# Attention and a two-layer MLP on one core: Silu table behind batch 1's Exp, eight banks for the first two tiles, a third q and k buffer

## The chip, the cores and the metric

One core of a Trainium2 chip runs the whole computation. The metric is the device time of one execution in microseconds (us), the median of several runs. The engines work side by side, each through its own list of instructions in order: TensorE (PE in the profile: matmuls; PEld: its weight loads), VectorE (DVE), ScalarE (ACT: activations and copies), GpSimd (POOL: here it issues nearly all loads) and SyncE (SP: here it issues the stores). Matmuls write into PSUM, which has 8 banks of 128 x 512 fp32 values.

## The reference

Sliding-window causal attention over 8 batches of 8 heads, 576 positions and 64 dimensions a head, then an MLP with Silu over the 4608 resulting tokens:

```python
batch, n_heads, seq, head_dim = (8, 8, 576, 64)
scores = scale * np.matmul(q, k.transpose(0, 1, 3, 2))
rel = pos[:, None] - pos[None, :]
mask = (rel >= 0) & (rel < 64)
scores = np.where(mask, scores, -1000000000.0)
attn = np.exp(scores - max);  attn = attn / sum
attn_out = np.matmul(attn, v)                 # -> x: 4608 tokens of 512
h = x @ w_in                                  # 512 -> 2048
out = (h * (1.0 / (1.0 + np.exp(-h)))) @ w_out   # 2048 -> 512
```

## The kernel before

**Tiles.** A batch has 9 blocks of 64 positions (`NB`), so there are 72 blocks, and the MLP takes them in 9 tiles of 512 tokens (`TT`, `NTT`), eight blocks each. Matmuls are in bf16 with fp32 sums.

**Attention.** For a block of 64 queries the keys are the block itself and the one before. q and k are loaded with the cast to bf16 by POOL and turned so that the head dimension lies on partitions. Batch 0 does this with TensorE: rows land in `natbs`, are transposed into PSUM (`turn_first`, L284) and copied to `qt[0]`, `kt[0]` (`lift`, L291). All later batches load into `nats` (`load_rows`, L241, four loads for each of four parts) and are turned by VectorE (`turn_blocks`, L248) into `qt[b % NK]`, `kt[b % NK]`. `NK = 2` is the number of q and k buffers; a batch's turning waits until the last scores of batch `b - NK` are done. v goes to `vv[b % NV]`, three buffers (`load_v`, L255), with two copies that shift half of it to the other partitions (`shift_v`, L299 and L301).

After batch 0, blocks are taken in *visits* of three (48 scores and 48 values matmuls), later four (64 and 64): scores into four banks (`scores`, L334), four Exp on ScalarE (`expo`, L344), four mask products on VectorE (`masking`, L349), values (`values`, L368) into two or three banks, then reciprocal (L375), product (L378) and a transpose into `bridge` (L382, L387), which holds x for the MLP. Batch 0 is done in six smaller units (L313, L321, L341, L355).

**MLP.** The first layer of a tile (`first_layer`, L393) makes 16 parts of 128 hidden features, four matmuls each, into one bank; ScalarE's Silu (L399) takes the bank to a `g` buffer in SBUF. Tile 0 also covers the ninth block of batch 0, in pieces of 192, 384, 256 and 320 columns; tile 1 goes in pieces of 192, 256 and 448 columns, and small copies (L402) bring over what tile 0 made for it. The second layer (`second_layer`, L405) is 4 x 16 matmuls of 512 columns into four banks; for tile 0 the hidden part is the outer loop, so all four banks fill together, and every eight matmuls need another block of w_out. An output copy (L411, on ScalarE or VectorE) and a store on SP (L415) follow.

**Order of the work.** The instructions are not issued as the code runs. `Plan` collects operations with a class (its rank in `rank`, `rank0` or `ahead`), an estimated duration on each engine that may do them, dependencies, a latency, a `gate` and a pool of PSUM banks; `Plan.run` plays them through in time and writes each engine's list in the order that comes out. An engine on the chip then follows its list strictly, waiting at each instruction for what it needs. Estimates therefore set the order, not the time. Pools: `at` banks 0 to 3, `pv` 4 and 5, `mp` and `pv3` 4 to 7, `all` all eight. The scores of a visit use `at`; values of batch 1 use `at` while few have been made and `pv` later; the first layer and the second use `mp`, until all values are made, and then all eight.

**Around the change.** ScalarE needs a table for Exp and another for Silu; a load of one replaces the other. A `prime` operation, a Silu over four values, draws the Silu table in behind batch 0's last Exp (L688). Later loads stand in front of the first Exp or Silu that needs another table. `add_first_batch` loads batch 0, `add_batch_qk` and `add_four` the others, `add_unit` makes batch 0's units, `add_visit` the visits, `add_tile` a tile's MLP. Instructions on PE in the order of the program before, from tile 0's second layer on, with the number of matmuls:

```
L405 x23, L334 x48, L405 x13, L334 x48, L405 x9, L334 x48, L405 x5, L368 x48, L405 x14,
L393 (192) x8, L368 x48, L393 (192) x16, L368 x48, L393 (192) x32, (256) x56, (448) x8,
L334 x48, L405 x21, L368 x48, L334 x48, L405 x27, L368 x48, L405 x2, L334 x64, L405 x14, L393 (512) x64
```

Of the kernel before, what the change touches and what calls it, by code (L numbers as in the profile page):

```python
# [122 lines left out]
def kernel(ctx, tc, q, k, v, w_in, w_out, out):  # L123
# [35 lines left out]
    nats = [keep.tile([128, 2 * S], BF16, name=f"nat{i}") for i in range(NN)]  # L159
    natbs = [keep.tile([128, S], BF16, name=f"natb{i}") for i in range(NNB)]  # L160
    qt = [keep.tile([128, NP * S], BF16, name=f"qt{i}") for i in range(NK)]
    kt = [keep.tile([128, 64 + NP * S], BF16, name=f"kt{i}") for i in range(NK)]
    vv = [keep.tile([128, H * NB + 1, D + 2], BF16, name=f"vv{i}") for i in range(NV)]
# [13 lines left out]
        rank=dict(prime=-8, early=-10, one=-9, edge=-8.5, first=-9, dma=-1, ld0=-1, dma0=-8.7, st=-2, silu=-3, out=-2, pv=0, s=1, moe=99, warm=200, turn=2,  # L177
                  norm=0, inverse=0, bridge=0, exp=1, mask=1, lift=2, block=2, shift=2, cast=4, rest=3, late=5, clear=9),
        rank0=dict(turn=-6, cast=-6, lift=-5, shift=-4.5, exp=-4, mask=-4, inverse=-3.5, norm=-3, bridge=-3.2),
# [272 lines left out]
    def add_first_batch():  # L452
        got = {}
        for what, u in FIRST_LOADS:
            if what == "v":
                add_v_loads(0, [u], [c_vv[0]])
                continue
            kk = "qk".index(what)
            w = n_nat[1] % NNB
            n_nat[1] += 1  # L460
            if u == 0:
                i = n_nat[0] % NN
                n_nat[0] += 1
                ld = p.add("ld0", {"SP": 0.45}, lambda _, i=i, kk=kk: load_first(i, kk), dma=-0.15 if kk == 0 else 0.7)
                ca = p.add("cast", {"ACT": 0.7, "DVE": 0.56}, lambda e, i=i, w=w: cast_first(e, i, w), [ld])
                nat_free[i] = [ca]
            else:
                ca = p.add("early" if (what, u) in FIRST_LOADS[2:6] else "dma0", {"POOL": 0.6}, lambda _, w=w, u=u, kk=kk: load_first_cast(w, u, kk), dma=0.74)
# [34 lines left out]
    def add_v_loads(b, parts, busy):  # L503
        v_landed.setdefault(b, []).extend(
            p.add("dma", {"POOL": 1.0}, lambda e, part=part: load_v(e, b, part), busy, dma=1.0 if b == 0 else 1.1, lat=MARGIN * (b > 0)) for part in parts)
# [64 lines left out]
    def add_visit(blocks):  # L570
# [3 lines left out]
        parts = [[(x, a) for x in range(min(w, 3))] for a in range(2)] + [[(3, 0), (3, 1)]] * (w == 4)  # L574
        n, e = len(g_pv), n_e[0]
        n_e[0] += 4
# [7 lines left out]
        for i in range(4):  # L584
            ex = p.add("exp", {"ACT": 0.39 + 0.1 * (w - 3)}, lambda _, i=i: expo(s["bank"][i], e + i, w), [s], lat=0.2, table="exp", b=b)
            s["untils"][i].append(ex)
            ready.append(p.add("mask", {"DVE": 0.37 + 0.1 * (w - 3)}, lambda _, i=i: masking(e + i, w, first), [ex, *c_mask], b=b))
# [11 lines left out]
        for c in all_b:  # L599
            s_last[c], pv_last[c] = [s], [pv]  # L600
        at = b * NB + blocks[0][1]
        for i, units in enumerate(parts):
            if i < 2:
                add_bank(pv, i, len(units), lambda _, n=n + i, a=i, k=len(units): to_bridge(n, at, a, k), range(at, at + len(units)), "", b)
            else:
                add_bank(pv, i, 2, lambda _, n=n + i: to_bridge_both(n, at + 3), [at + 3], "", b)
# [6 lines left out]
    def add_tile(j):  # L613
# [18 lines left out]
        for i, (ft, lo, hi) in enumerate(work):  # L632
# [19 lines left out]
        for i, (m, f, lo, hi) in enumerate(order):  # L652
# [29 lines left out]
    for lo, hi in ((0, 256), (256, 512), (512, 1024), (1024, 1536), (1536, 2048)):  # L682
        landed = [p.add("dma", {"POOL": 0.6}, lambda _, a=a, lo=lo, hi=hi: load_w_in(a, lo, hi), dma=1.31 * (hi - lo) / 512)
                  for a in range(2)]
        win.extend([landed] * ((hi - lo) // 128))
    add_batch_attention(0)

    p.add("prime", {"ACT": 0.2}, lambda _: nc.scalar.activation(out=spare, in_=zero, func=ACTF.Silu), [c_zero] + exps[0],  # L688
          table="silu")
    n_tile = 0  # L690
    for b in range(1, B):
# [42 lines left out]
```

## Time and profile before

| what | value |
|---|---|
| median of 4 runs | 297.98 us (297.35, 297.48, 298.48, 298.51) |
| the profiled execution, its own time | 297.48 us |
| its span, first to last instruction | 295.7 us |
| mean granted TensorE clock | 1.000 |
| table loads on ScalarE | 1.28 us each |

The profile is a record of one execution: a page of sums, and views that can be asked of its trace. A line of a timeline reads: start in us from the span's start, length in us, engine, line of the kernel, operation, what it writes and reads, number of instructions merged; in brackets, if the engine was idle before it, how long and what ended the idle time. A line of the windows reads: window, its length, then busy time (and number of instructions) of PE, PEld, DVE, ACT and POOL, the granted clock, the share of the DMA engines and GB/s. The ends of matmuls are modelled, so one starts before another ends; the starts tell more.

The DMA share is 1.3 to 1.9 in every window up to 66.5 us, and POOL issues its loads in the same stretch nearly without a pause.

### The profile page before, as it was taken

The page shows a single profiled execution, that of the slowest core. Times are in us where ns is not written, and L with a number is a line of the kernel's source. Part 1 is how long each engine was busy: PE and PEld are TensorE (multiplying, and loading weights), DVE is VectorE, ACT ScalarE, POOL GpSimd, SP SyncE. Part 2 cuts the span into 40 slices and gives each one's busy share as a digit, 9 for nine tenths or more (in the row PEclk, how much of TensorE's full clock was granted, in tenths as well). Part 3 has the DMA queues.
Part 4 walks back from the last instruction along what each step waited for, and adds up shares of the span by engine and source line. Part 5 has one row for each costly group of instructions (what it writes and reads, how often), then busy time and mean ns, then how long its engine had stood idle before and what let it go on. Part 6 is the DMA issues. An engine that isn't in the chain of part 4 may idle for free.

```text
span 295.7 us, 8520 instructions
## 1 busy us (share of the span) xinstructions
PE 288.4 (98%) x3641; PEld 150.8 (51%) x3641; DVE 142.3 (48%) x344; ACT 168.9 (57%) x316; POOL 118.1 (40%) x175
## 2 busy tenths in 40 slices
PE   8979999899999999999999999999999999999996
PEld 4556644775444555455544544455444444444444
DVE  3882478978894577847791990066504000000000
ACT  4878655887377646673477338744872166217512
POOL 8967896979899979960400000000000000000000
PEclk9999999999999999999999999999999999999999
DMA  8999999999999999992590120012100200010012
GB/s 161 174 198 173 147 169 171 228 134 137 178 184 138 117 181 170 144 105 74 65 91 0 38 75 35 1 38 75 38 0 30 78 35 2 35 71 35 3 71 72
DMA packets 82982, 28.64 MB, mean 97 GB/s; under 512 B 72448, under 2 KB 78208, under 8 KB 82944
## 3 DMA queue, kind: packets, MB, share of 16 engines
q0 software_dynamic: 77184, 18.07, 66.2%
q1 hardware_dynamic: 5760, 10.03, 9.4%
q8 instruction: 28, 0.46, 0.6%
q14 instruction: 10, 0.08, 0.1%
HBM read 36.70 MB, written 9.44 MB: 156 GB/s over the span
## 4 chain that ended last, share of the span: by engine, by line
PE 83%; POOL 8%; DMA 5%; issue 1%; ACT 1%; POOLq 0%; ACTq 0%
PE mp L405 31%; PE mp L393 30%; PE at L405 9%; PE at L393 6%; PE at L334 3%; DMA w_in_sb<-in_moe_w_in_dram 3%; PE mp L368 3%; POOL w_in_sb L261 2%; POOL nat L241 2%; POOL vv L255 2%; DMA w_out_sb<-in_moe_w_out_dram 2%; POOL natb L231 1%; POOL w_out_sb L267 1%; ACT ot L411 0%; ACT g L399 0%
## 5 line engine op out<-in xcount | busy, mean ns | idle before, releaser
L393 PE MATMUL mp<-bridge,w_in_sb 128*128 128x512 bf16 (+5 forms) x612 | 109.8, 337 | 2.7 <-DMA w_in_sb<-in_moe_w_in_dram 1.2
L405 PE MATMUL mp<-w_out_sb,g 128*128 128x512 bf16 x448 | 101.7, 379 | 0.5 <-DMA w_out_sb<-in_moe_w_out_dram 0.5
L393 PEld LDWEIGHTS <-w_in_sb 128*128 128x128 bf16 x696 | 66.6, 98 | 61.7 <-issue 2.3
L399 ACT ACTIVATE g<-mp 128x512 bf16<-128x512 f32 (+5 forms) x153 | 77.2, 513 | 26.6 <-PE mp L393 25.4
L405 PEld LDWEIGHTS <-g 128*128 128x128 bf16 x608 | 56.6, 98 | 63.1 <-issue 1.0
L344 ACT ACTIVATE e<-at 128x512 bf16<-128x512 f32 (+1 forms) x68 | 33.0, 572 | 16.0 <-PE at L334 15.9
L241 POOL DMA_DIRECT2D nat<-in_k_dram x56 | 35.5, 650 | 9.4 <-DMA vv<-in_v_dram 4.4
L255 POOL DMA_DIRECT2D vv<-in_v_dram x32 | 31.9, 1016 | 15.4 <-PE mp L368 13.7
L411 ACT COPY ot<-mp 128x512 f32<-128x512 f32 x20 | 11.6, 587 | 44.3 <-PE mp L405 22.1
L241 POOL DMA_DIRECT2D nat<-in_q_dram x56 | 34.4, 633 | 3.5 <-DMA w_in_sb<-in_moe_w_in_dram 2.1
L375 DVE RECIPROCAL rc<-mp 128x6 f32<-128x6 f32 (+1 forms) x47 | 8.1, 185 | 53.0 <-PE mp L368 52.3
L405 PE MATMUL at<-w_out_sb,g 128*128 128x512 bf16 (+2 forms) x160 | 28.4, 336 | 0.0
L349 DVE TENSOR_TENSOR e<-e,masks 128x512 bf16<-128x512 bf16 (+1 forms) x68 | 23.4, 392 | 1.8 <-ACT e L344 1.6
L248 DVE STREAM_TRANSPOSE kt<-nat 128x576 bf16<-128x576 bf16 x28 | 20.7, 785 | 7.0 <-DMA nat<-in_k_dram 7.0
L248 DVE STREAM_TRANSPOSE qt<-nat 128x576 bf16<-128x576 bf16 x28 | 20.9, 789 | 3.5 <-DMA nat<-in_q_dram 3.4
L378 DVE TENSOR_TENSOR ox<-mp,rc 128x384 bf16<-128x384 f32 (+1 forms) x47 | 21.7, 510 | 0.1
L382 DVE STREAM_TRANSPOSE bridge<-ox 128x384 bf16<-128x384 bf16 x40 | 20.7, 553 | 0.0
L393 PE MATMUL at<-bridge,w_in_sb 128*128 128x512 bf16 x84 | 19.3, 379 | 0.0
L411 ACT COPY ot<-at 128x512 f32<-128x512 f32 (+2 forms) x10 | 5.0, 500 | 22.4 <-PE at L405 22.4
L399 ACT ACTIVATE g<-at 128x512 bf16<-128x512 f32 x21 | 12.5, 597 | 5.7 <-PE at L393 5.7
L368 PEld LDWEIGHTS <-e 128*32 128x32 bf16 x1008 | 9.6, 94 | 6.7 <-issue 5.4
L334 PE MATMUL at<-qt,kt 32*128 32x64 bf16 x1008 | 11.1, 191 | 0.0
(63 smaller groups left out, 135.2 us busy)
## 6 DMA issues: line engine op xcount, KB each, us to landing
out_dram<-ot SPq DMA_DIRECT2D x35, 256.0 KB, 2.6
vv<-in_v_dram POOLq DMA_DIRECT2D x32, 144.0 KB, 5.4
nat<-in_q_dram POOLq DMA_DIRECT2D x56, 72.0 KB, 3.9
nat<-in_k_dram POOLq DMA_DIRECT2D x56, 72.0 KB, 3.7
w_out_sb<-in_moe_w_out_dram POOLq DMA_DIRECT2D x8, 256.0 KB, 6.1
w_in_sb<-in_moe_w_in_dram POOLq DMA_DIRECT2D x6, 256.0 KB, 8.0
w_in_sb<-in_moe_w_in_dram POOLq DMA_DIRECT2D x4, 128.0 KB, 5.1
natb<-in_q_dram POOLq DMA_DIRECT2D x3, 144.0 KB, 5.5
```

Source lines behind the costliest of these rows:

```text
L241: nc.gpsimd.dma_start(out=nats[i][32 * h:32 * h + 32].rearrange("p (m x) -> p m x", m=NB), in_=(q, k)[kk][b, 4 * a + h].rearrange("(m p r) ...
L248: nc.vector.transpose(out=to[:, (2 * a + part) * S:(2 * a + part + 1) * S].rearrange("x (m t r) -> x m r t", t=32, r=2), in_=nats[i].rearr ...
L255: queue[e].dma_start(out=vv[b % NV][:, 2 * g0 + 1:2 * g1 + 1:2, 0:D], in_=v[b].rearrange("h s d -> (h s) d").rearrange("(g p) d -> p g d", ...
L334: nc.tensor.matmul(banks[op["bank"][h]][:, (2 * x + a) * 64:(2 * x + a + 1) * 64], lhsT=kt[b % NK][r, at:at + 128], rhs=qt[b % NK][r, at:a ...
L344: nc.scalar.activation(out=es[e % NE][:, 0:128 * n], in_=banks[bank][:, 0:128 * n], func=ACTF.Exp, scale=scale)
L349: nc.vector.tensor_mul(at, at, masks[:, i:i + n].rearrange("k x h i -> k (x h i)"))
L368: nc.tensor.matmul(at_pv(bank)[32 * h:32 * h + 32, u, t], lhsT=es[(e + h) % NE][:, at:at + 32], rhs=vv[b % NV][:, (4 * a + h) * NB + i, 0: ...
L378: nc.vector.tensor_mul(oxs[n % NOX][:, 0:w], at_pv(bank)[:, 0:w, :, 0:D], rcs[n % NRC][:, 0:w].unsqueeze(3).to_broadcast([128, w, 2, D]))
L382: nc.vector.transpose(out=bridge[:, n0:n0 + w, 2 * a:2 * a + 2].rearrange("x t s (u i) -> x t s u i", u=2), in_=oxs[n % NOX][:, 0:w].rearr ...
L393: nc.tensor.matmul(banks[bank["bank"][0]][:, 0:hi - lo], lhsT=w_in_sb[:, c, ft * 128:(ft + 1) * 128], rhs=bridge[:, (j * TT + lo) // 64:(j ...
L399: nc.scalar.activation(out=gts[gt][:, lo:hi], in_=banks[bank["bank"][0]][:, 0:hi - lo], func=ACTF.Silu)
L405: nc.tensor.matmul(banks[bank["bank"][0]][:, 0:hi - lo], lhsT=gts[gt][:, m * 128:(m + 1) * 128], rhs=w_out_sb[:, f, lo:hi], start=(f == 0) ...
```

## The change

- **Silu table.** `prime` becomes a function `load_silu(b)` that is called behind batch 0 as before and once more behind batch 1's attention; it depends on the batch's Exp operations, which `add_visit` now collects in `exps`.
- **Banks.** The first layer's pool is `all` for tiles 0 and 1 and `mp` from tile 2 on. Tile 0's output copies are offered to ScalarE alone.
- **Batch 1's values.** Their pool is `at` throughout; a gate in the planner lets a visit's values run only when the previous values were placed more than `APART` = 2.4 planned us ago. Batch 1's masks get a class of their own, `mask1`, with a rank ahead of other VectorE work, and its first visit's reciprocal, product and bridge are in the class that goes ahead (`"0"`).
- **Third buffer.** `NK` is 3. A tile `third` holds what `natbs` held (batch 0's rows), and the same space is the third `qt` and `kt`.
- **Estimated latencies.** Batch 0's loads get 0.7 (`CAL`) more, w_in's 0.6 or 1.4.

```diff
-    NK = 2
+    NK = 3
+    APART = 2.4
+    CAL = 0.7
-    natbs = [keep.tile([128, S], BF16, name=f"natb{i}") for i in range(NNB)]
-    qt = [keep.tile([128, NP * S], BF16, name=f"qt{i}") for i in range(NK)]
-    kt = [keep.tile([128, 64 + NP * S], BF16, name=f"kt{i}") for i in range(NK)]
+    third = keep.tile([128, 64 + 2 * NP * S], BF16, name="third")
+    natbs = [third[:, i * S + 64 * (i >= NP):(i + 1) * S + 64 * (i >= NP)] for i in range(NNB)]
+    qt = [keep.tile([128, NP * S], BF16, name=f"qt{i}") for i in range(NK - 1)] + [third[:, 0:NP * S]]
+    kt = [keep.tile([128, 64 + NP * S], BF16, name=f"kt{i}") for i in range(NK - 1)] + [third[:, NP * S:64 + 2 * NP * S]]
-                  norm=0, inverse=0, bridge=0, exp=1, mask=1, lift=2, ...
+                  norm=0, inverse=0, bridge=0, exp=1, mask=1, mask1=-1.5, lift=2, ...
-    ... load_first_cast(w, u, kk), dma=0.74)
+    ... load_first_cast(w, u, kk), dma=0.74, lat=CAL)
-            p.add("dma", ..., busy, dma=1.0 if b == 0 else 1.1, lat=MARGIN * (b > 0)) for part in parts)
+            p.add("dma", ..., busy, dma=1.0 if b == 0 else 1.1, lat=MARGIN if b else CAL) for part in parts)
-        for a, z in ([(i, i + 1) for i in range(NP)] if b < NK else [(0, NP)]):
+        for a, z in ([(i, i + 1) for i in range(NP)] if b < NIV else [(0, NP)]):
+            exps.setdefault(b, []).append(ex)
-            ready.append(p.add("mask", ...
+            ready.append(p.add("mask" if b > 1 else "mask1", ...
-                   gate=values_may_run if b > 1 else None,
-                   pool="pv3" if b > 1 else "pv" if n > 6 else "at", b=b, nb=len(parts))
+                   gate=values_may_run if b > 1 else lambda last=pv_last[b - (at == b * NB)][0]: last["seen"] is not None and p.now > last["at"] + APART,
+                   pool="pv3" if b > 1 else "at", b=b, nb=len(parts))
-                add_bank(..., range(at, at + len(units)), "", b)
+                add_bank(..., range(at, at + len(units)), *(("0", 0) if at == NB else ("", b)))
-                           pool=None if c else "mp")
+                           pool=None if c else "mp" if j > 1 else "all")
-                cp = p.add("out", {"DVE": 0.18 + (hi - lo) / 1000, "ACT": 0.18 + (hi - lo) / 1160},
+                cp = p.add("out", {"ACT": 0.18 + (hi - lo) / 1160, **({"DVE": 0.18 + (hi - lo) / 1000} if j else {})},
-        landed = [p.add("dma", {"POOL": 0.6}, ..., dma=1.31 * (hi - lo) / 512)
+        landed = [p.add("dma", {"POOL": 0.6}, ..., dma=1.31 * (hi - lo) / 512, lat=0.6 if hi <= 512 else 1.4)
-    p.add("prime", {"ACT": 0.2}, ... ACTF.Silu), [c_zero] + exps[0], table="silu")
+    def load_silu(b):
+        p.add("prime", {"ACT": 0.2}, ... ACTF.Silu), [c_zero] + exps[b], table="silu")
+    load_silu(0)
         add_batch_attention(b)
+        if b == 1:
+            load_silu(1)
```

The order on PE in the program after, from the same place:

```
L405 x18, L334 x48, L405 x15, L334 x48, L405 x9, L334 x48, L405 x5, L368 x48, L405 x9, L368 x48, L405 x8,
L393 (192) x2, L368 x48, L393 (192) x54, (256) x56, (448) x8,
L334 x48, L405 x18, L368 x48, L334 x48, L405 x21, L368 x48, L405 x25, L393 (512) x64, L334 x64, L405 x21
```

More of the change, by code (lines that the diff above doesn't have):

```diff
@@ L177 @@
         rank=dict(prime=-8, early=-10, one=-9, edge=-8.5, first=-9, dma=-1, ld0=-1, dma0=-8.7, st=-2, silu=-3, out=-2, pv=0, s=1, moe=99, warm=200, turn=2,
-                  norm=0, inverse=0, bridge=0, exp=1, mask=1, lift=2, block=2, shift=2, cast=4, rest=3, late=5, clear=9),
+                  norm=0, inverse=0, bridge=0, exp=1, mask=1, mask1=-1.5, lift=2, block=2, shift=2, cast=4, rest=3, late=5, clear=9),
         rank0=dict(turn=-6, cast=-6, lift=-5, shift=-4.5, exp=-4, mask=-4, inverse=-3.5, norm=-3, bridge=-3.2),
@@ L467, in add_first_batch @@
             else:
-                ca = p.add("early" if (what, u) in FIRST_LOADS[2:6] else "dma0", {"POOL": 0.6}, lambda _, w=w, u=u, kk=kk: load_first_cast(w, u, kk), dma=0.74)
+                ca = p.add("early" if (what, u) in FIRST_LOADS[2:6] else "dma0", {"POOL": 0.6}, lambda _, w=w, u=u, kk=kk: load_first_cast(w, u, kk), dma=0.74, lat=CAL)
             got[what, u] = (w, ca)
@@ L504, in add_v_loads @@
         v_landed.setdefault(b, []).extend(
-            p.add("dma", {"POOL": 1.0}, lambda e, part=part: load_v(e, b, part), busy, dma=1.0 if b == 0 else 1.1, lat=MARGIN * (b > 0)) for part in parts)
+            p.add("dma", {"POOL": 1.0}, lambda e, part=part: load_v(e, b, part), busy, dma=1.0 if b == 0 else 1.1, lat=MARGIN if b else CAL) for part in parts)
     def add_batch_v(b):
@@ L574, in add_visit @@
         parts = [[(x, a) for x in range(min(w, 3))] for a in range(2)] + [[(3, 0), (3, 1)]] * (w == 4)
-        n, e = len(g_pv), n_e[0]
+        n, e, at = len(g_pv), n_e[0], b * NB + blocks[0][1]
         n_e[0] += 4
@@ L586, in add_visit @@
             s["untils"][i].append(ex)
-            ready.append(p.add("mask", {"DVE": 0.37 + 0.1 * (w - 3)}, lambda _, i=i: masking(e + i, w, first), [ex, *c_mask], b=b))
+            exps.setdefault(b, []).append(ex)
+            ready.append(p.add("mask" if b > 1 else "mask1", {"DVE": 0.37 + 0.1 * (w - 3)}, lambda _, i=i: masking(e + i, w, first), [ex, *c_mask], b=b))
         g_mask.append(ready)
         pv = p.add("pv", {"PE": 0.1 + 0.147 * w}, None, ready + [d for b in all_b for a in range(2) for d in v_done[(b, a)]], lat=0.1,
-                   gate=values_may_run if b > 1 else None,
-                   pool="pv3" if b > 1 else "pv" if n > 6 else "at", b=b, nb=len(parts))
+                   gate=values_may_run if b > 1 else lambda last=pv_last[b - (at == b * NB)][0]: last["seen"] is not None and p.now > last["at"] + APART,
+                   pool="pv3" if b > 1 else "at", b=b, nb=len(parts))
         for i in range(4):
@@ L600, in add_visit @@
             s_last[c], pv_last[c] = [s], [pv]
-        at = b * NB + blocks[0][1]
         for i, units in enumerate(parts):
             if i < 2:
-                add_bank(pv, i, len(units), lambda _, n=n + i, a=i, k=len(units): to_bridge(n, at, a, k), range(at, at + len(units)), "", b)
+                add_bank(pv, i, len(units), lambda _, n=n + i, a=i, k=len(units): to_bridge(n, at, a, k), range(at, at + len(units)), *(("0", 0) if at == NB else ("", b)))
             else:
@@ L682 @@
     for lo, hi in ((0, 256), (256, 512), (512, 1024), (1024, 1536), (1536, 2048)):
-        landed = [p.add("dma", {"POOL": 0.6}, lambda _, a=a, lo=lo, hi=hi: load_w_in(a, lo, hi), dma=1.31 * (hi - lo) / 512)
+        landed = [p.add("dma", {"POOL": 0.6}, lambda _, a=a, lo=lo, hi=hi: load_w_in(a, lo, hi), dma=1.31 * (hi - lo) / 512, lat=0.6 if hi <= 512 else 1.4)
                   for a in range(2)]
@@ L686 @@
     add_batch_attention(0)
-    p.add("prime", {"ACT": 0.2}, lambda _: nc.scalar.activation(out=spare, in_=zero, func=ACTF.Silu), [c_zero] + exps[0],
-          table="silu")
+    def load_silu(b):
+        p.add("prime", {"ACT": 0.2}, lambda _: nc.scalar.activation(out=spare, in_=zero, func=ACTF.Silu), [c_zero] + exps[b],
+              table="silu")
+    load_silu(0)
     n_tile = 0
```

## The prediction

> **What bounds the kernel now.** I read the page first, then the table of windows, the chain of waits and, because the chain passes through several engines only between 40 and 57 us, the timelines of TensorE, ScalarE and VectorE there.
>
> ```profile
> span 295.7 us, 8520 instructions
> PE 288.4 (98%) x3641; PEld 150.8 (51%) x3641; DVE 142.3 (48%) x344; ACT 168.9 (57%) x316; POOL 118.1 (40%) x175
> ```
>
> ```profile
> 66.50:293.00 226.50, 226.33 (x2720) 110.61 (x2720) 99.35 (x233) 122.45 (x207) 64.16 (x92) 1.00 0.56 75
> ```
>
> From 66.5 us TensorE is busy for 226.33 of 226.50 us at a granted clock of 1.00. What the change does to the order of work there can win nothing; time can only be won before. The chain gives the rate: `83.31 13.81 PE mp L393 x64` is 64 matmuls of 512 columns, 0.2158 us each. TensorE's timeline before:
>
> ```profile
> 20.23 14.37 PE L393 MATMUL mp<-bridge,w_in_sb 128*128 128x192 bf16 x110 [1.23 <-DMA w_in_sb<-in_moe_w_in_dram]
> 34.43 5.16 PE L405 MATMUL mp<-w_out_sb,g 128*128 128x512 bf16 x23
> 39.53 0.55 PE L334 MATMUL at<-qt,kt 32*128 32x64 bf16 x48
> 40.01 2.12 PE L405 MATMUL mp<-w_out_sb,g 128*128 128x512 bf16 x9
> 42.66 1.02 PE L405 MATMUL mp<-w_out_sb,g 128*128 128x512 bf16 x4 [0.53 <-DMA w_out_sb<-in_moe_w_out_dram]
> 43.61 0.55 PE L334 MATMUL at<-qt,kt 32*128 32x64 bf16 x48
> 44.09 2.12 PE L405 MATMUL mp<-w_out_sb,g 128*128 128x512 bf16 x9
> 46.14 0.55 PE L334 MATMUL at<-qt,kt 32*128 32x64 bf16 x48
> 46.62 1.25 PE L405 MATMUL mp<-w_out_sb,g 128*128 128x512 bf16 x5
> 47.81 0.56 PE L368 MATMUL at<-vv,e 128*32 128x65 bf16 x48
> 48.30 3.19 PE L405 MATMUL mp<-w_out_sb,g 128*128 128x512 bf16 x14
> 51.52 0.82 PE L393 MATMUL mp<-bridge,w_in_sb 128*128 128x192 bf16 x8
> 52.27 0.56 PE L368 MATMUL mp<-vv,e 128*32 128x65 bf16 x48
> 53.65 1.73 PE L393 MATMUL mp<-bridge,w_in_sb 128*128 128x192 bf16 x16 [0.82 <-ACT g L399]
> 55.31 0.56 PE L368 MATMUL mp<-vv,e 128*32 128x65 bf16 x48
> ```
>
> Starts show what the modelled ends hide: a start later than the one before it plus its work is a wait. I call the 64 second-layer matmuls of tile 0 (L405) by number, 0 to 63; every eight need another block of w_out. Two more rows matter:
>
> ```profile
> 51.97 1.28 ACT L399 ACT_TABLE_LOAD   x1
> ```
>
> ```profile
> 38.20 1.50 DVE L248 STREAM_TRANSPOSE kt<-nat 128x576 bf16<-128x576 bf16 x2 [5.19 <-DMA nat<-in_k_dram]
> ```
>
> The first is the Silu table, in front of tile 1's first Silu. The second is the turning of batch 1's last k rows, which landed at 38.08 by the trace of the DMAs; it ends at 39.70, just in time for the first scores (L334, 39.53 to 40.01, whose second half of matmuls needs it).
>
> **The price list of 40.01 to 56.72 us.** Scores: after nine L405 from 44.09 TensorE would be free at 46.03, and the next L405 starts at 46.62, so a block of 48 scores costs 0.59. Values (L368): five L405 from 46.62 end at 47.70, the next starts at 48.30, 0.60. First layer: the chain has 88 matmuls (24 of 192, 56 of 256, 8 of 448 columns) from 56.72 to 66.33 without a wait, 9.61 us for 22,528 columns, so 0.082 for 192. The work from 40.01 to 56.72 is then 41 L405 (8.85), two blocks of scores (1.18), three of values (1.79) and 32 first-layer matmuls (2.62): 14.44 of 16.71 us. TensorE waits 2.27:
> - 0.70 at 42.66, for w_out's fifth block, which landed at 42.61 (nine L405 from 40.01 end at 41.96);
> - 0.20 before 51.52 (14 L405 from 48.30 end at 51.32), for a bank that an output copy still holds;
> - 0.89 before 53.65 (values from 52.27 end near 52.76): two output copies at 50.88 to 51.95, the table load, then the first Silu, all on ScalarE, while the next banks are full;
> - 0.25 each near 54.5 and 56.7, where the chain goes through a Silu (54.17, 56.34): four banks are too few.
>
> **The change, part by part.**
>
> *Silu table behind batch 1's Exp, and all eight banks for tiles 0 and 1.* ScalarE's number of instructions grows by one dummy activation (0.21 by the L688 row); the table loads stay 14. The load now follows the twelfth Exp of batch 1 in ScalarE's order. That Exp ends near 48.1 (third scores end near 46.4, four Exp take 1.64), the load at 49.4. The output copies cannot begin before matmul 60 at about 51.7, so over 2 us cover the load. If the cover went, the first Silu would move by the uncovered part. Eight banks remove the 0.20 and both 0.25; together with the load the last four waits go, 1.59 in all. The other way: a bank lent to the first layer must be free for scores. Batch 1's scores come 4 us after the last Silu of tile 0's first layer (35.1), and batch 2's scores use banks whose Silu ends about 1 us before; nothing is charged, between 0 and one Silu (0.5).
>
> *Tile 0's output copies on ScalarE alone.* Three copies stand before tile 1's first Silu instead of two, 0.54 each by the 50.88 row (two in 1.07): from 51.7 to 53.3, first Silu done near 53.7. TensorE needs that bank again after five others, near 54.6. Cost nothing, cover 0.9. The Trainium skill (ScalarE: Activation LUTs, Rules for kernel authors) speaks against it: simple element-wise work belongs on VectorE. The rows differ: VectorE's two copies at 51.10 took 1.29, ScalarE's two 1.07. By the rule these copies would be slower than before, by the rows they are not, and either way the 0.9 covers them. The same page (What ACT_TABLE_LOAD costs) gives 1.28 us plus a drain of 1.38. The trace has the next Silu at 53.27, 0.02 after the load; by the page the removed wait would be larger by 1.38, which this case does not show.
>
> *Batch 1's values spaced, in the scores' banks, and masks first.* The order of the instructions, which can be read without running, puts the blocks of 48 so: scores after 18, 33 and 42 L405, values after 47, 56 and, the third, after all 64 and two first-layer matmuls. The number of blocks is unchanged, and over the whole program as many values as before (12) are followed directly by scores. So no block's price changes, only its place.
>
> *The first scores move from after 23 L405 to after 18.* This is the part that costs. TensorE gets there at 34.43 + 18 x 0.2158 + 0.04 (a short wait at 34.9 in the trace) = 38.36, but the turned k is ready at 38.95 (first half) and 39.70. TensorE works in order, so 46 L405 queue behind it. VectorE's and POOL's orders up to there are the old ones, the loads do not depend on TensorE, so I keep 39.70: scores end near 39.95, L405 number 18 starts at 40.05, where before number 23 started at 40.01. Five L405, 1.08 us, are left over. In exchange the wait for w_out goes: number 32 is reached at 43.08, after the block's 42.61; number 40 at 45.4 (lands 44.93), 48 at 48.3 (47.08), 56 at 50.6 (48.83).
>
> *The head (CAL, mask1, w_in's later dates in the planner, batch 0's bridge ahead).* It moves instructions, four more warming matmuls among them, but tile 0's first layer waits at 18.8 to 20.23 for half of w_in, landed at 20.18 in a queue of loads that the change leaves in order. Replaying the new order with the old rows I get tile 0's last bridge at 21.5 instead of 20.94, needed at 21.7. Even if late, the wall at 39.70 leaves TensorE 1.0 more. Charged 0, between 0 and 0.5.
>
> *Third q and k buffer.* Batch 0's rows lie in it first, each slice with its own waits. From batch 2 on VectorE may turn rows a batch earlier; TensorE waits for none of it in the 226 us. Worth 0. Its danger is on VectorE, below. Batch 2's third scores and values also move behind tile 2's first layer: same price, later place.
>
> *Sum.* After: from 40.05, 46 L405 (9.93), 1.18, 1.79 and 2.62 make 15.52, so the point that was at 56.72 is reached at 55.57: 1.15 earlier (1.59 + 0.70 - 1.08, less rounding and the 0.04). What follows is packed, so the end moves as much: span 294.55, and 297.48 - 1.15 = 296.33 for the profiled execution. Its 297.48 is 0.50 under the median of 297.98 (two runs lie near 297.4, two near 298.5); taking the difference from the median gives **296.8 us**. 0.3%, about what a measurement of this kernel can tell from no change, is 0.9 us: faster begins below 297.1, so the forecast stands only just on that side.
>
> **Rivals.**
> - *No wall at the first scores.* If k's rows are turned by 38.4, only w_out holds TensorE, to 42.66; from there 32 L405 (6.91), 1.18, 1.79, 2.62 make 12.50, 55.16 instead of 56.72: 1.56, **296.4**. For it: an execution with faster loads would do it, since nothing else holds these rows. Against: the landing at 38.08, in a stretch where the DMA engines hardly rest.
> - *The head eats it.* The new order puts two blocks of batch 0's scores before the second turning of k, so the Exps, values and bridges end later. Cover 0.2 at 21.7 and 1.0 at the wall; lateness beyond 1.2 is paid one for one, and from 1.5 to 2.3 late the result is within 0.3%: **297.5**.
> - *VectorE's order turns against it (slower).* At batch 2's first values VectorE now does the v shift (landed 64.87, work to 66.6), two turnings of batch 3's q (to 68.11 by the old rows) and four masks in a row (1.32, to 69.43), and TensorE comes after 18 L405 instead of 21: 65.18 + 0.59 + 3.88 + 0.1 = 69.75. The cover is 0.3, where it was about 0.7 (masks done 70.86, values at 71.54). Everything behind is paid one for one: if those loads, which share the DMA engines with tile 0's output stores, land 1.45 later, the gain is gone; from 2.35 it is slower by 0.3%, at 3 us late **298.7**. Against: the stores start later too, and the fourth comes after the Silus.
>
> **How the numbers follow.** Forecast 0.50 (own range 296.2 to 297.4: the 0.5 of the head or of a bank, and as much the other way), no wall 0.12, head 0.20, VectorE 0.18. Faster: 0.38 of the forecast's 0.50 and the 0.12; slower: 0.16 of VectorE's; the rest is within 0.3%. The range is 295.9 to 298.5: from a little below the second case to most of the fourth.
>
> **What would show it.** The first scores of batch 1 start after 18 L405 and are stretched, ending near 40; no wait for w_out at 42.7; a table load near 48, none near 52; no TensorE gap between 50 and 57; batch 2's first scores near 65.2 instead of 66.4; everything behind without gaps. Wrong if k's rows land much earlier or later than 38.1, if tile 0's second layer starts after 35.4, or if a gap appears before batch 2's values near 69.7.

## The result, and the profile after

| | median, us | runs | ratio to before, 95% interval |
|---|---|---|---|
| before | 297.51 (296.36 to 300.42) | 59 | |
| after | 298.46 (296.88 to 301.22) | 38 | 1.0028, 1.0015 to 1.0042 |

Predicted were 296.8 us and a gain; the change made the kernel slower by 0.28%. That is little, but the whole interval lies above 1. (The ratios here compare all fast runs; they are not the quotients of the medians, here 1.0032.) The profiled execution took 297.65 us, one of the faster ones. Its page and one row of its windows:

```profile
span 295.8 us, 8535 instructions
PE 288.0 (97%) x3645; PEld 150.7 (51%) x3645; DVE 140.1 (47%) x341; ACT 170.6 (58%) x321; POOL 117.5 (40%) x175
```

```profile
66.60:293.00 226.40, 226.32 (x2721) 110.60 (x2720) 98.87 (x231) 122.93 (x207) 62.82 (x91) 1.00 0.56 75
```

From 66.6 us TensorE is packed, as before from 66.5. So in this execution all that was won ahead of that point was also lost ahead of it. TensorE's timeline there (three lines have been added ahead of the functions, so before's L334, L368, L393, L405 are now L337, L371, L396, L408):

```profile
34.73 4.08 PE L408 MATMUL mp<-w_out_sb,g 128*128 128x512 bf16 x18
38.75 0.65 PE L337 MATMUL at<-qt,kt 32*128 32x64 bf16 x28
39.72 0.32 PE L337 MATMUL at<-qt,kt 32*128 32x64 bf16 x20 [0.32 <-DVE kt L251]
39.97 3.41 PE L408 MATMUL mp<-w_out_sb,g 128*128 128x512 bf16 x15
...
48.00 2.12 PE L408 MATMUL mp<-w_out_sb,g 128*128 128x512 bf16 x9
50.05 0.45 PE L371 MATMUL at<-vv,e 128*32 128x65 bf16 x33
51.66 0.30 PE L371 MATMUL at<-vv,e 128*32 128x65 bf16 x15 [1.17 <-issue]
51.90 1.90 PE L408 MATMUL mp<-w_out_sb,g 128*128 128x512 bf16 x8
53.63 0.33 PE L396 MATMUL at<-bridge,w_in_sb 128*128 128x192 bf16 x2
```

The wall at the turned k stands where it was predicted (39.72), the wait for w_out is gone, the waits for banks and for Silu's table are gone. The table load is on ScalarE at 48.10:

```profile
48.10 1.28 ACT L692 ACT_TABLE_LOAD   x1
```

What is new is a stop in the middle of a block of values: 33 matmuls run, 15 follow 1.17 us later. The list of TensorE's waits (waiting engine and line, what ended the wait, us in total, times, longest) says of it

```profile
PE at L371 <- issue: 1.2, 1, 1.2
```

"issue" is time in which the engine waited for nothing that the profile shows: no data, no bank, no semaphore. Batch 2's first scores start at 66.57 (66.42 before). Without the stop they would have come near 65.4, and the prediction had 65.2.

### The profile page after: what moved, and what is told of

It reads as the page before. It is cut to its first block, busy times and chain, and to the rows that moved or that the text cites. A ratio compares the mean times of both kernels' runs of the same rounds, so it can differ in the third digit from the quotient of the medians.

```text
span 295.8 us, 8535 instructions
## 1 busy us (share of the span) xinstructions
PE 288.0 (97%) x3645; PEld 150.7 (51%) x3645; DVE 140.1 (47%) x341; ACT 170.6 (58%) x321; POOL 117.5 (40%) x175
## 4 chain that ended last, share of the span: by engine, by line
PE 85%; POOL 7%; DMA 5%; issue 1%; DVE 0%; ACT 0%; POOLq 0%; DVEq 0%; ACTq 0%
PE mp L408 32%; PE mp L396 29%; PE at L408 9%; PE at L396 8%; PE at L337 3%; DMA w_in_sb<-in_moe_w_in_dram 3%; PE mp L371 3%; POOL w_in_sb L264 2%; POOL nat L244 2%; DMA nat<-in_k_dram 2%; POOL vv L258 1%; POOL third L234 1%; PE at L371 1%; POOL w_out_sb L270 0%; DVE kt L251 0%
## 5 line engine op out<-in xcount | busy, mean ns | idle before, releaser
L408 PE MATMUL mp<-w_out_sb,g 128*128 128x512 bf16 x448 | 101.5, 379 | 0.0
L396 PE MATMUL mp<-bridge,w_in_sb 128*128 128x512 bf16 (+5 forms) x476 | 97.3, 357 | 1.3 <-DMA w_in_sb<-in_moe_w_in_dram 1.3
L396 PEld LDWEIGHTS <-w_in_sb 128*128 128x128 bf16 x696 | 66.6, 98 | 59.5 <-DMA w_in_sb<-in_moe_w_in_dram 1.5
L408 PEld LDWEIGHTS <-g 128*128 128x128 bf16 x608 | 56.5, 98 | 62.3 <-issue 0.2
L402 ACT ACTIVATE g<-mp 128x512 bf16<-128x512 f32 (+5 forms) x119 | 64.6, 552 | 23.3 <-PE mp L396 22.8
L414 ACT COPY ot<-mp 128x512 f32<-128x512 f32 x23 | 13.3, 588 | 45.4 <-PE mp L408 21.8
L244 POOL DMA_DIRECT2D nat<-in_k_dram x56 | 34.3, 628 | 11.1 <-DMA vv<-in_v_dram 4.2
L396 PE MATMUL at<-bridge,w_in_sb 128*128 128x512 bf16 (+4 forms) x220 | 37.1, 311 | 0.0
L402 ACT ACTIVATE g<-at 128x512 bf16<-128x512 f32 (+4 forms) x55 | 24.9, 461 | 7.0 <-PE at L396 6.5
L408 PE MATMUL at<-w_out_sb,g 128*128 128x512 bf16 (+2 forms) x160 | 28.4, 336 | 0.0
L381 DVE TENSOR_TENSOR ox<-mp,rc 128x384 bf16<-128x384 f32 (+1 forms) x45 | 20.5, 507 | 0.1
L251 DVE STREAM_TRANSPOSE kt<-nat 128x576 bf16<-128x576 bf16 x20 | 14.9, 790 | 7.5 <-DMA nat<-in_k_dram 7.5
L251 DVE STREAM_TRANSPOSE qt<-nat 128x576 bf16<-128x576 bf16 x20 | 14.7, 786 | 4.4 <-DMA nat<-in_q_dram 4.3
L371 PEld LDWEIGHTS <-e 128*32 128x32 bf16 x1008 | 9.7, 94 | 8.2 <-issue 6.1
L251 DVE STREAM_TRANSPOSE third<-nat 128x576 bf16<-128x576 bf16 x16 | 11.5, 784 | 1.0 <-PE at L337 1.0
```

The lines of the kernel that those rows point to most:

```text
L244: nc.gpsimd.dma_start(out=nats[i][32 * h:32 * h + 32].rearrange("p (m x) -> p m x", m=NB), in_=(q, k)[kk][b, 4 * a + h].rearrange("(m p r) ...
L251: nc.vector.transpose(out=to[:, (2 * a + part) * S:(2 * a + part + 1) * S].rearrange("x (m t r) -> x m r t", t=32, r=2), in_=nats[i].rearr ...
L371: nc.tensor.matmul(at_pv(bank)[32 * h:32 * h + 32, u, t], lhsT=es[(e + h) % NE][:, at:at + 32], rhs=vv[b % NV][:, (4 * a + h) * NB + i, 0: ...
L381: nc.vector.tensor_mul(oxs[n % NOX][:, 0:w], at_pv(bank)[:, 0:w, :, 0:D], rcs[n % NRC][:, 0:w].unsqueeze(3).to_broadcast([128, w, 2, D]))
L396: nc.tensor.matmul(banks[bank["bank"][0]][:, 0:hi - lo], lhsT=w_in_sb[:, c, ft * 128:(ft + 1) * 128], rhs=bridge[:, (j * TT + lo) // 64:(j ...
L402: nc.scalar.activation(out=gts[gt][:, lo:hi], in_=banks[bank["bank"][0]][:, 0:hi - lo], func=ACTF.Silu)
```

## The experiments

Three views gave the first theory. The profile's page has a DMA queue of a kind of its own, the same in both kernels, and a window of the DMA view around 49.3 us holds one packet of it (packets, MB, share of the 16 engines):

```profile
q8 instruction: 28, 0.46, 0.6%
```

```profile
q8 instruction: 1, 0.02, 6.2%
```

28 packets, 0.46 MB: 16 KB each, for TensorE's 7,290 instructions (3,645 matmuls, each with a weight load), so about 256 instructions a packet. In the trace of the DMAs that packet starts at 49.30, and TensorE goes on at 51.66, 2.36 us later. The third view counts how far TensorE had come; the second number in parentheses is its weight loads:

```profile
0.00:51.60 51.60, 46.79 (x734) 27.89 (x735) 29.60 (x89) 35.17 (x80) 42.53 (x68) 1.00 1.44 171
```

**Theory F: TensorE had run out of instructions.** The change puts two blocks of 48 values, 192 instructions that take 1 us, with only nine L408 between them. The next packet would be asked for when TensorE enters the packet before, and come late in a stretch where the DMA engines hardly rest. **Theory D**: something that the second values need is late and the profile doesn't name it.

**Shift the count.** Small matmuls that compute nothing of the result go in front of tile 0's fifth group, where TensorE waits for w_in.

```diff
     def first_layer(bank, j, ft, c, lo, hi):
+        if (j, ft, c, lo) == (0, 4, 0, 0):
+            for i in range(46):    # 80 in before_80
+                nc.tensor.matmul(banks[bank["bank"][0]][32 * (i % 4):32 * (i % 4) + 32, 0:8],
+                                 lhsT=blank[:, 0:32], rhs=blank[:, 0:8], start=True, stop=True)
```

> The changed kernel with 46 very small matmuls (128x32 by 128x8, 92 instructions) before tile 0's fifth first-layer group, where TensorE then waits about 1.3 us for w_in anyway; nothing else moves. Theory F (TensorE had not yet got its next 256 instructions): the place of the stop is fixed by the number of instructions before it, so it moves 46 matmuls earlier, from behind matmul 33 of the second block of values to behind matmul 44 or so of the first block (near 47.8 us), and the second block runs through. TensorE gets there sooner after the last such point than it did, so the stop is at least as long: 1.5 to 3.5 us, ratio to before 1.004 to 1.012. Theory D (the second values wait for data, a bank or masks that the profile does not name): the stop stays behind matmul 33 of the second values, 1.2 us, ratio as the changed kernel, 1.003. Theory N (the small matmuls cost by themselves): tile 0's second layer starts later than 34.73 by as much as is lost.

> The kernel before with the same 46 small matmuls at the same place. Theory F: a stop appears that the kernel before does not have, behind matmul 45 or so of the first block of values (near 48 us), 1 to 3 us, and the time grows by as much, less what the waits behind it (w_out is past, Silu's table 0.89) hide: ratio 1.002 to 1.009. Theory D: nothing but the small matmuls' own cost, hidden in the wait for w_in: ratio 1.000, no new stop. Theory N: as D, with the second layer later by what is lost.

> The control: the kernel before with 80 small matmuls there (160 instructions). Theory F: the points at which TensorE takes up new instructions fall where it gets there more slowly than at any of the two others (8.1 us from one to the next at the shortest), so no stop of 0.3 us or more between 40 and 60 us; ratio 1.000, at most 1.002 if the small matmuls outlast the wait for w_in. Theory N: slower than the kernel with 46, by 80/46 of its loss. Theory D: ratio 1.000.

Ratios 1.0104 (1.0057 to 1.0152), 1.0077 (1.0045 to 1.0109) and 1.0011 (0.9979 to 1.0043). The timeline and the count of after_46, then of before_46:

```profile
48.09 0.52 PE L371 MATMUL at<-vv,e 128*32 128x65 bf16 x44
50.15 0.21 PE L371 MATMUL at<-vv,e 128*32 128x65 bf16 x4 [1.54 <-issue]
```

```profile
0.00:50.10 50.10, 44.83 (x734) 27.25 (x735) 27.16 (x82) 34.87 (x79) 40.04 (x63) 1.00 1.41 170
```

```profile
51.80 0.54 PE L368 MATMUL at<-vv,e 128*32 128x65 bf16 x45
53.26 0.21 PE L368 MATMUL at<-vv,e 128*32 128x65 bf16 x3 [0.92 <-issue]
```

```profile
0.00:53.20 53.20, 47.05 (x734) 28.71 (x735) 27.75 (x82) 33.61 (x77) 43.00 (x69) 0.94 1.41 168
```

The stop moved back by exactly 46 matmuls (4 + 9 + 33), into another block, and the kernel before, which had none, got one. In all three it stands behind 735 weight loads. before_80, the control, has no such stop between 40 and 60 us. That is F; D falls, since different data are read there. What these runs show is the place of the stop, not its price: after_46's trace is the fastest of its six runs, that of before_46 the second slowest of twelve. The ratios are not clean either: the small matmuls themselves hold such a point, behind 351 weight loads (735 less three times 128), and TensorE stopped there for 1.4 us in after_46, 2.7 in before_46 and 1.1 in before_80; the wait for w_in, 1.2 to 1.3 us, hides the last of these alone. What the 2.7 cost besides, the granted clock of before_46 shows (the number behind the five engines; 1.00 in both windows in the kernel before):

```profile
21.60:24.50 2.90, 2.87 (x50) 2.71 (x50) 0.00 (x0) 0.99 (x3) 1.39 (x2) 0.50 1.41 193
24.50:29.00 4.50, 4.50 (x21) 2.29 (x19) 1.19 (x3) 2.30 (x7) 3.50 (x6) 0.64 1.41 163
```

**Space the blocks.** In the changed kernel: `APART = 4.0` (apart_40), or the gate's 2.4 replaced by one number for the second visit and another for the third (4.0 and 1.6 in g_40_16, 3.2 and 2.4 in g_32_24).

> The changed kernel with batch 1's values spaced by 4.0 us in the planner instead of 2.4: the second block of values comes behind 16 second-layer matmuls instead of 9, the third behind 39 first-layer matmuls instead of 2; the rest of the order is nearly the same. Theory F: TensorE takes about 1.5 us longer to the point where it stopped, so the stop of 1.2 us shrinks below 0.3 and the gain that the prediction summed appears: span about 294.6, ratio to before 0.995 to 0.998. Theory D: what the second values wait for is also ready by then, if it was only late by 1.2; the same gain, so this run does not tell D from F, but both from a cause that lies elsewhere (third buffer, head): then ratio stays at 1.003.

> The changed kernel with only the second block of batch 1's values put later (behind 16 second-layer matmuls instead of 9) and the third behind 19 first-layer matmuls of 192 columns, 20 fewer than in the run with 4.0 us for both; the rest of the order is that of the changed kernel. Theory F (the stop is TensorE waiting for its next 256 instructions): the second block comes 1.5 us later, so no stop above 0.3 us at instruction 1479; the third block's bridge comes 1.6 us earlier than in that run, so its wait of 0.57 us is gone too. Span about 294.6, ratio to before 0.995 to 0.998. Rival W: what that run lost before 45 us (the turned k 0.44 later, w_out 0.66 later) comes from the order and not from that execution; then it comes again, span near 296, ratio 1.000 to 1.004.

> The same with the second block behind 13 second-layer matmuls and the third behind 14 first-layer matmuls. Theory F: 0.86 us more for the instructions, so of the stop of 1.2 us some 0.3 is left in an execution like the profiled one; ratio to before 0.996 to 0.999. Rival W: 1.000 to 1.004.

No trace of the three stops behind 735 loads any more, as F had it. But the gain didn't come: 1.0060 (1.0032 to 1.0087), 1.0002 (0.9977 to 1.0028), 1.0001 (0.9973 to 1.0029). In apart_40 the third block of values was too late for tile 1, a wait of 0.57 for its bridge, but that and later loads explain its profiled execution only; what put half of its runs above 300 us was not seen. The traces of the other two lost their time to loads that landed late, as rival W has it: TensorE waited 0.85 us for a shift of v and 0.24 for w_out in g_40_16, 1.26 for w_out in g_32_24. So the stop was not all.

**Parts alone, on the kernel before.** b_silu has only `load_silu(1)` behind batch 1, b_silu_all also the pool `all` for tiles 0 and 1.

> The kernel before with the Silu table's place alone changed (loaded behind batch 1's Exps). The prediction's term: 0.89 us at 53.65, less what the three short waits for banks behind it then grow by. Theory F: no stop at instruction 1479. Span about 294.9, ratio 0.996 to 0.999. Rival: the wait only moves to the next Silu or bank; ratio 1.000.

> The kernel before with two parts of the change alone: Silu's table loaded behind batch 1's Exps, and all eight banks for tiles 0 and 1. The blocks of values stay spaced as before (the second behind 14 second-layer and 10 first-layer matmuls), the third comes behind 30 first-layer matmuls. The prediction's terms for these parts: 0.89 for the table and 0.70 for the banks, 1.59 in all, with the wait for w_out (0.70) still there. Theory F: TensorE has as long for instruction 1479 as before, less the short waits, so no stop there; span about 294.2, ratio 0.994 to 0.997. Rival: the third values' bridge comes too late for tile 1's second columns, as it did at 59 us with the values spaced by 4.0; then 0.5 to 1 us of it is lost, ratio 0.997 to 1.000.

0.9966 (0.9947 to 0.9986) and 0.9973 (0.9950 to 0.9996), no stop in either trace. The wait for the table was real and worth about what was charged. The banks added nothing that shows beside it: the gain of b_silu_all is 0.8 us, its interval ends at 1.5, and the prediction's two terms make 1.59. In its trace the four waits behind 50 us are gone, but 0.86 us was lost to a block of w_out near 48 us and 0.36 to a Silu.

**Which part of the change costs.** after_again is the changed kernel; a_nk2 has `NK = 2` and batch 0's rows in `natbs` again; a_lat takes `CAL`, 0.6 and 1.4 out of the planner; al_36_16 is a_lat with 3.6 and 1.6 in the gate.

> The changed kernel itself once more, on another chip and with another profiled execution. Theory F: TensorE stops again at instruction 1479 (behind matmul 33 of the second block of values), for 0 to 3 us, and goes on about 2.3 us after the 16 KB packet of instructions starts; ratio to before 1.001 to 1.005. Rival W (what is lost are loads that land late, and the stop was one execution's accident): no stop there, the loss lies in waits for w_out, v or k between 38 and 50 us.

> The changed kernel with the third q and k buffer undone (two buffers, batch 0's rows in a space of their own as before); TensorE's order up to 66 us is the same, instruction for instruction. Theory F: the stop at instruction 1479 stays, ratio as the changed kernel, 1.002 to 1.004. Rival T (the third buffer's extra transfers or VectorE's turned order cost the time): ratio 0.996 to 0.999.

> The changed kernel with the planner's later landing dates (CAL, 0.6 and 1.4 for w_in) undone: the head is instruction for instruction that of before, the first scores stand behind 23 second-layer matmuls again, the second values still behind 9 after the first, the third behind 14 first-layer matmuls. Theory F: instruction 1479 is again inside the second block of values and TensorE has 0.7 us more for its instructions at most (the wait for w_out comes back), so a stop of 0.3 to 1.2 us stays; ratio 0.999 to 1.003. Rival W (the early first scores cost it): ratio 0.995 to 0.998, and no stop.

> The same with batch 1's values spaced as before the change: the second block behind 14 second-layer and 1 first-layer matmul, the third behind 16 first-layer matmuls; so the change without its early first scores and without its closer second values. Theory F: no stop at instruction 1479; the table's 0.89 and the banks' 0.70 come out, the wait for w_out stays; ratio 0.994 to 0.998, as the run with two parts alone (0.9973). Rival T: the third buffer takes it back; ratio 1.000 to 1.003.

0.9995 (0.9965 to 1.0025), 1.0026 (1.0003 to 1.0049), 0.9979 (0.9951 to 1.0007), 0.9979 (0.9955 to 1.0003). The traces of the first three stop behind 735 weight loads, the fourth doesn't. The third buffer is not the cause. The planner's dates, which move the head and the first scores, are under suspicion: without them the ratio is 0.9979 whether the trace has the stop or not, though both intervals just reach 1.

**Head or first scores.** b_lat is the kernel before with the planner's dates alone. a_s10 is the changed kernel with batch 1's first scores behind 23 second-layer matmuls again. al_e3 is a_lat with one more edit, which brings the first scores behind 18 and leaves the head as before (the first values then come behind 11 L408 instead of 5, the second behind 9 as in the change):

```diff
-                    dma=0.42, lat=MARGIN) for h in range(4)]
+                    dma=0.42, lat=MARGIN if b > 1 else 0.3) for h in range(4)]
```

> The kernel before with the planner's later landing dates alone (0.7 for batch 0's rows and v, 0.6 and 1.4 for w_in): the head takes the order of the changed kernel, the first scores come behind 18 second-layer matmuls, the second values behind 17 second-layer and 8 first-layer matmuls. Theory H (this part is what costs): ratio 1.002 to 1.004, tile 0's second layer 0.3 to 0.7 us later than 34.43, no stop at instruction 1479. The prediction's terms for it: head 0, wall at the first scores 1.08, w_out wait saved 0.70; 0.4 us, ratio 1.001. Theory F alone: no stop, ratio 1.000.

> The changed kernel with batch 1's first scores put behind 23 second-layer matmuls again, the new head kept; second values behind 9 after the first. If the head costs: ratio 1.001 to 1.004, as the changed kernel. If the early first scores cost: ratio 0.996 to 0.999, as the run with both undone (0.9979). Theory F: the stop at instruction 1479 falls behind matmul 28 of the second values, in the same executions as before.

> The changed kernel with the old head, but batch 1's first scores behind 18 second-layer matmuls (k's landing date in the planner 1.0 us earlier). If the early first scores cost: ratio 1.001 to 1.004. If the head costs: 0.996 to 0.999. Theory F: stop at instruction 1479 behind matmul 33 of the second values.

> The changed kernel itself a third time, on the chip of these runs. Theory F: TensorE stops at instruction 1479 again and goes on 2.2 to 2.5 us after the start of the 16 KB packet; first layer from about 17.5, second layer from 34.7 or later; ratio 1.000 to 1.004.

1.0063 (1.0039 to 1.0086), 1.0015 (0.9993 to 1.0036), **0.9950 (0.9932 to 0.9968)**, 1.0038 (1.0014 to 1.0061). b_lat holds both, the new head and the early first scores. The clearest comparison is al_e3 against after_third, on the same chip: with the old head the early first scores gain, with the new head they lose. With the late first scores the heads differ the same way (a_s10 1.0015, a_lat 0.9979), but those intervals overlap. So the new head costs, the early first scores don't. b_lat and al_e3 were repeated:

> The kernel before with the planner's later landing dates alone, once more. If the loss of a typical execution lies in the head: tile 0's last bridge ends at 21.5 or later (20.94 before), the second layer starts at 35.2 or later or with matmuls at half the granted clock behind the pause for w_in near 20 us, and from 40 us on the trace is like that of before. If it lies behind: the head as in the first trace, and a stop or waits of 1 us or more between 40 and 60 us. Ratio 1.003 to 1.008 in either case.

> The changed kernel with the old head and the first scores behind 18 second-layer matmuls, once more. If the head is what cost, ratio 0.993 to 0.997 as in the first run, the last bridge at 20.9 to 21.0 us, the second layer from 34.0 to 34.6; if the first run's chip made it, 0.997 to 1.001.

1.0035 (1.0007 to 1.0062) and 0.9947 (0.9924 to 0.9970). The version al_e3 beats both kernels: medians 296.33 and 296.59, its first profiled span 294.1. It passes the point behind 735 loads 2.4 and 3.2 us after its packet's start, without a stop. Over the study every kernel with the new head has a ratio of 0.9995 or more, every one with the old head and any part of the change 0.9979 or less.

**Where the head's loss sits.** Not where the expectation of b_lat_2 looked. Its second layer starts at 34.46 (34.43 before), and its clock is 1.00. Its span is 2.6 us longer than that of the kernel before. 0.8 of it is lost ahead of 67 us, where TensorE waited 0.74 for w_out and 0.63 for a Silu. The rest is one stop. Its timeline and count near 117 us, then those of the kernel before:

```profile
115.76 0.38 PE L393 MATMUL mp<-bridge,w_in_sb 128*128 128x512 bf16 x1
117.72 1.46 PE L393 MATMUL mp<-bridge,w_in_sb 128*128 128x512 bf16 x6 [1.58 <-issue]
```

```profile
0.00:117.66 117.66, 111.10 (x1758) 64.55 (x1759) 79.59 (x194) 77.21 (x161) 99.85 (x150) 1.00 1.48 164
```

```profile
114.94 4.26 PE L393 MATMUL mp<-bridge,w_in_sb 128*128 128x512 bf16 x19
```

```profile
0.00:115.95 115.95, 111.56 (x1758) 64.86 (x1759) 79.36 (x193) 75.57 (x160) 100.25 (x151) 1.00 1.49 165
```

It is the same stop, 1,024 weight loads (eight times 128) behind the first. The new head has four more warming matmuls, so each such point comes four matmuls earlier in the program: here behind one matmul of the first layer instead of five, 0.86 us sooner. The kernel before gets there 2.34 us after the packet's start, just in time; b_lat_2 has to wait for it. b_lat, of which the trace is the fastest run of twelve, stops there for 0.1 only. The changed kernel has its own such place, behind 2,143 loads. after_third, whose trace is the slowest of its twelve runs, first the waits that matter, then timeline and count:

```profile
PE mp L396 <- issue: 2.0, 1, 2.0
PE at L337 <- DVE kt L251: 1.6, 2, 1.3
PE at L371 <- issue: 1.3, 1, 1.3
```

```profile
147.30 0.38 PE L396 MATMUL mp<-bridge,w_in_sb 128*128 128x512 bf16 x1
149.64 1.67 PE L396 MATMUL mp<-bridge,w_in_sb 128*128 128x512 bf16 x7 [1.97 <-issue]
```

```profile
0.00:149.58 149.58, 139.75 (x2126) 79.51 (x2143) 100.70 (x238) 95.86 (x194) 114.55 (x171) 1.00 1.34 149
```

al_e3, with the old head, runs over the same point:

```profile
143.83 5.34 PE L396 MATMUL mp<-bridge,w_in_sb 128*128 128x512 bf16 x24
```

```profile
0.00:144.85 144.85, 139.43 (x2126) 79.31 (x2143) 98.77 (x234) 95.27 (x195) 114.33 (x171) 1.00 1.37 153
```

The account of after_third's 299.7 us of span: the predicted 294.55, plus 1.85 because its k was turned late (L408 restarts at 41.90, not 40.05), plus the stops of 1.3 and 2.0, makes 299.70. That of the profiled execution: 294.55, less 0.08 at the wall (39.97), plus 1.2, makes 295.67 of 295.8.

Of the traces without small matmuls, ten have the new head and seven the old one. Behind 66 us, five of the ten stop for 0.3 to 2.0 us at the end of a packet, none of the seven for more than 0.2. But the second layer also starts later, at 34.5 to 35.2 us in nine of the ten against 34.0 to 34.6, so the shift of the packets is not all that differs.

## Why the prediction was wrong

- *What bounds the kernel, the price list, the four waits and w_out's:* right. The waits went, and up to 50.05 us the trace runs as the sum says; in the other traces of this order w_out cost 0.2 to 0.4 us again. With the old head the total comes out: 294.1 and 295.0 of span against 294.55, though that they lie evenly around it is luck. al_e3's k was turned at 38.4, so it ran without the wall, and its 294.1 is what the first rival gives (295.7 - 1.56); al_e3_2 had the wall (L408 restarts at 39.87). The banks' 0.70 was not seen by itself (b_silu_all).
- *"The first scores move from after 23 L405 to after 18. This is the part that costs."* The wall was priced right (40.05 predicted, 39.97 measured), and the part with its early scores is in the fastest version.
- *"So no block's price changes, only its place."* This is the step that failed. A block of 48 costs 0.59 only if its instructions are there. From the end of one packet (behind 607 loads) TensorE came to the end of the next in 4.3 us, where the kernel before takes 6.2; the packet after that had not arrived, and it paid 0.2 to 1.3 us in all four traces of this order (the changed kernel's three and a_nk2). The nine L408 alone don't decide: al_e3 and a_s10 have them too, but took 6.2 and 4.9 us, and in a_s10 the packet started sooner, 1.8 us after that end against 3.4.
- *The head, "It moves instructions, four more warming matmuls among them", "Charged 0":* the second failure. The late bridge and second layer (34.73) were indeed covered by the wall. What was not looked at is that four matmuls more move all later packet ends. The planner's dates alone, head and early first scores together, cost 0.35 and 0.63%, and one of their two traces shows a stop of 1.6 us where the kernel before passes just in time. A kernel with only four warming matmuls more or fewer was not run, so how much of the head's cost is this shift, and how much its other order, is argued, not shown.
- *"What follows is packed, so the end moves as much":* true of the order, not of every execution; in after_third 2.0 us are lost at 147 us.
- *ScalarE's copies, banks lent to the first layer, third buffer, at 0:* no trace shows a loss from them; a_nk2 clears the third buffer.
- *The rivals.* VectorE's order did not hold batch 2's values (no wait there). "The head eats it" has the right place and the wrong reason: its time came near, through instructions, not through late bridges. None of them named instructions. VectorE's rival also has a slip: 3 us late is 2.7 beyond the cover, so by its own figures 296.8 + 2.7 = 299.5 and not 298.7. The range's upper end, 298.5, goes back to it, and that the measured 298.46 still lies below that end is luck: that rival's condition did not come.
- *"What would show it"* named the gap that mattered: a gap between 50 and 57 us, and batch 2's scores at 66.57 instead of 65.2.
- Open: apart_40's slow half, and why spacing the values alone (g_40_16, g_32_24) gained so little in the median; their traces lost to late loads, and one of each does not say how often. g_32_24 passes the point behind 2,143 loads 2.33 us after its packet's start, so the next stop is near, but this trace has none there.

## What to carry over

A block of many small matmuls has a second price, its instructions. Find one mark (the end of a packet) from a stop, step on by 256 instructions from there, and ask how long TensorE takes from mark to mark. Here the marks lay behind 351, 735 or 1,759 weight loads, steps of 128, and not at whole multiples of 256 from the program's start. Whether the time is enough hangs on when the next packet starts, plus some 2.3 us: in the changed kernel's profiled execution 3.2 us were just enough at the 2,143 mark, where the packet started 0.9 us after TensorE had passed the mark before; 4.3 were 1.4 too few (1.17 of it shows as idle) at 735, where it started 3.4 after. A stop with "issue" in the middle of a block that has all its data may be this, and shifting the count by a known number of matmuls tests it. Instructions added anywhere, even idle warming ones, move every mark behind them.

## What the runs showed of the hardware

In twenty traces TensorE never passed the end of a packet less than 2.25 us after the next packet's start, and where it stopped it mostly went on 2.25 to 2.5 us after it, at the latest 3.35; the packet's own transfer takes 0.9 to 1.4 in nine of ten packets, up to 2.0 before a stop. In the changed kernel the packet of the 735 mark started 3.4 us after TensorE had passed the mark before (45.9 us). From 160 us on, with few loads left, it was 0.8 to 1.1 in five of ten packets, and the other five started 0.8 to 4.3 us ahead of that point. That the loads are what delays it is likely, not shown: no run took loads away. The Trainium skill (Runtime: NRT & Kernel Launch, Instruction fetch mechanics) states blocks of 16 KiB or 256 instructions that the sequencer fetches through a DMA queue of its own. The traces agree: 128 weight loads from mark to mark, 28 packets. It calls the cost of crossing a block "mostly hidden"; here a stop of 0.2 to 2.7 us stood at the end of a packet in twelve of the twenty traces, and the measurement decides. After a stop of 2.7 us the granted clock was 0.50 for the next 2.9 us and 0.64 for 4.5 more.
